# A convolution feeding a channel mix: the first x over two hardware queues, and the first two groups convolved together

## The chip, the cores and the metric

The kernel runs on one core of a Trainium2 chip. Each core has its own instruction streams: TensorE (PE, with its weight loads shown as PEld), VectorE (DVE), ScalarE (ACT), GpSimd (POOL) and SyncE (SP). SP, ACT and POOL can issue DMA transfers; those of SP and ACT are hardware queues, those of POOL a software queue, which can change the type of the data on the way. Matrix products go into PSUM, from where VectorE and ScalarE read them; the rest of the on-chip data lies in SBUF. The metric is the time of one execution on the device in microseconds (us), as a median over runs.

## The reference

`x` is 8 sequences of 4160 tokens with 192 channels, fp32. First a causal convolution over 7 tokens, whose weights are a softmax, one set for each of 8 heads of 24 channels; then a channel mix with a shift by one token.

```python
w = softmax(weight)                               # 8 heads x 7 taps
out = einsum('hk,bskhg->bshg', w, x_unfolded)     # causal, zeros ahead of token 0

x = out
x_prev = x shifted by one token, zeros first
xk = mu_k * x + (1.0 - mu_k) * x_prev
xr = mu_r * x + (1.0 - mu_r) * x_prev
k = np.maximum(xk @ w_k, 0.0)                     # 192 -> 1024
v = k * k @ w_v                                   # 1024 -> 192
r = 1.0 / (1.0 + np.exp(-(xr @ w_r)))
return r * v
```

## The kernel before

Sequences are worked on in four pairs. The tokens of a pair are cut into blocks of 120, and blocks into groups: in the first pair groups 0 to 5 have 3, 4, 4, 5, 10 and 9 blocks, and later pairs have larger ones. A group's life: `x_tile` takes a buffer `xb` out of three and clears what lies ahead of the first token; `load_x` loads it on POOL's queue and casts fp32 to bf16 on the way (lines 116 and 122); `conv` multiplies it with `toe`, a banded matrix for each head that holds the softmaxed weights (`conv_mm`, line 250), and copies the result out of PSUM to `y` (`conv_out`, lines 286 and 289). Then `y` must be turned so that channels lie on partitions: groups 0 to 3 by transposes on TensorE (`tr`, line 324) that VectorE copies to `yT` (line 334), the others by way of DRAM. Of `yT`'s three parts, two hold channels 0 to 127 of one sequence each, the third channels 128 to 191 of both.

The channel mix goes in steps of 512 tokens, the first one of 256. For a step, VectorE makes `diff` (line 355) and from it with `mix` the operand `xk` and later `xr` (lines 394 and 397: a product, then a sum). `k_mm` (line 416) multiplies `xk` with `wk` into PSUM tiles, one per slot: first the 128 high channels ("hi"), then the 64 low ones ("lo") of the two sequences. `k_relu` (line 457) on ScalarE reads a slot, `k_square` (line 476) on VectorE squares it, `v` (line 505) and `r` (lines 500, 501, 522) follow, and `v_out` multiplies and writes. The first step has four slots, the second eight; four slots are a bundle.

All PSUM tiles come from one `ring` of four, in the order in which they are asked for: a tile is used again only when its fourth predecessor has been read. Every engine works strictly in the order in which the program issues its instructions, and that order is written by hand: `prologue` (line 654) up to the first bundle, then the loop at line 710, which runs tables of functions (`early`, `first`, `xt`, `mixes`, `late` and others) entered by bundle number.

The prologue's order matters here. SP loads `w_raw`, the raw weights, then six small pieces of `mu`. POOL makes `ident`, issues the four transfers of group 0's x (lines 116 and 122), makes the mask `band`, and then issues group 1's x (two), `wk` (three, lines 158 to 160), group 2's x (two), `wr` (five), `wv` (line 170); two memsets follow (line 692), then x of groups 3 and 4. Each queue kind has eight semaphores for its transfers, so the ninth waits until the first has landed. VectorE and ScalarE turn `w_raw` into the softmax and `toe` (lines 173 to 224). ScalarE loads its table for Exp at the start (line 659) and the one for Sigmoid after it (line 179). TensorE runs `warm`, products of constants that nobody reads: 16 at first, then 4, 2 and 3 between the convolution of group 0 (8 products), its 9 transposes, and the convolution of group 1. Group 0's `y` is copied by `conv_out_first` in six pieces (lines 268 and 272).

In the first bundle the first two slots of K are computed (hi, then lo), then group 1 is transposed, then the other two slots follow; group 2 is convolved behind them, and K of the second step after that. In the second bundle come group 2's transposes and group 3's convolution.

Of the kernel before, what the change touches and what calls it, by code (L numbers as in the profile page):

```python
# [14 lines left out]
def kernel(  # L15
# [114 lines left out]


    w_raw = const.tile([P, H, K], FP32)
# [24 lines left out]
    def load_wk():  # L157
        nc.gpsimd.dma_start(out=wk[:, 0, :], in_=moe_w_k[0:P, :])
        nc.gpsimd.dma_start(out=wk[0:LO, 1, :], in_=moe_w_k[P:D, :])
        nc.gpsimd.dma_start(out=wk[LO:P, 1, :], in_=moe_w_k[P:D, :])  # L160
# [11 lines left out]
    def softmax():  # L172
        nc.vector.tensor_reduce(out=w_max, in_=w_raw, axis=mybir.AxisListType.X, op=ALU.max)
        nc.vector.tensor_tensor(
            out=w_exp, in0=w_raw, in1=w_max.unsqueeze(2).to_broadcast([P, H, K]), op=ALU.subtract
        )
        nc.scalar.activation(out=w_exp, in_=w_exp, func=AF.Exp)

        nc.scalar.activation(out=w_sig, in_=w_exp[:, 0, 0:1], func=AF.Sigmoid)
        nc.vector.tensor_reduce(out=w_sum, in_=w_exp, axis=mybir.AxisListType.X, op=ALU.add)  # L180
        nc.vector.reciprocal(out=w_sum, in_=w_sum)
        nc.vector.tensor_tensor(
            out=w_nrm,
            in0=w_exp,
            in1=w_sum.unsqueeze(2).to_broadcast([P, H, K]),
            op=ALU.mult,
        )
# [52 lines left out]
    def conv_mm(g, c):  # L240
        nb = groups[g][2]
        if c == 0 and g > 0:
            ys[g] = two.tile([P, GB, 2 * D], BF16, tag="y", name="y")
# [14 lines left out]
    def conv_out_first():  # L258

        nb = groups[0][2]  # L260
        ys[0] = [const.tile([P, nb, P], BF16, tag=f"y0{i}", name="y0") for i in range(3)]
        for c, hs in enumerate(chunks(0)):
            ps = conv_ps.pop((0, c))
            c0, c1 = hs[0] * G, hs[-1] * G + G
            n = min(c1, P) - c0
            if n > 0:
                for i, copy in enumerate((nc.scalar.copy, nc.vector.tensor_copy)):
                    copy(out=ys[0][i][:BLK, :, c0 : c0 + n], in_=ps[:BLK, :, i, 0:n])
            if c1 > P:
                n = c1 - max(c0, P)  # L270
                lo = ys[0][2][:BLK, :, :].rearrange("p n (s c) -> p n s c", s=2)
                nc.scalar.copy(out=lo[:, :, :, c1 - P - n : c1 - P], in_=ps[:BLK, :, :, c1 - c0 - n : c1 - c0])
# [41 lines left out]
    def tr(g, j):  # L314

        p, blk0, nb, _, _ = groups[g]
        if blk0 == 0 and j == 0:
            new_yT(p)
# [3 lines left out]
        for c in range(3):  # L322
            for i in todo:
                nc.tensor.transpose(
                    out=view[:, (i - 4 * j) // 2, c, i % 2, :],
                    in_=ys[g][c][:BLK, i, :] if g == 0 else ys[g][:BLK, i, c * P : (c + 1) * P],
                    identity=ident[:BLK, :BLK],
                )

        def evacuate(cs):  # L330
            for i in todo[::2]:
                n = min(2, nb - i)
                c0 = YC + (blk0 + i) * BLK
                nc.vector.tensor_copy(
                    out=yTs[p][:, cs, c0 : c0 + n * BLK].rearrange("p c (n t) -> p c n t", n=n),
                    in_=view[:, (i - 4 * j) // 2, cs, :n, :],
                )

        if g > 0:
            evacuate(slice(0, 3))  # L340
        else:
            for part, cs in enumerate((slice(0, 2), slice(2, 3))):
                evacuate(cs)
                diff(0, cs)
                mix(0, 0, part)
# [16 lines left out]
    def mix(s, i, part):  # L362
# [28 lines left out]
        else:  # L391
            sl = slice(0, 2) if part == 0 else slice(2, 3)
            o = t[:, sl, :L]
            nc.vector.tensor_scalar(  # L394
# [6 lines left out]
    def k_mm(n, hi, start):  # L401
# [5 lines left out]
        if start:  # L407
            k_ps[n] = ring.tile([P, 2, BANK], FP32, tag="k", name="ps_k")
# [15 lines left out]
    def k_section(ns):  # L424
# [4 lines left out]
        h = len(ns) // 2 if ns[0] > 0 else len(ns)  # L429
# [158 lines left out]
    def conv(g, c):  # L588
        conv_mm(g, c)
        for k in range(c, min(c + 2, len(chunks(g)))):  # L590
            conv_out(g, k, nc.scalar.copy)

    for g, (p, blk0, nb, fb, on_pe) in enumerate(groups):
        nx = -(-len(chunks(g)) // 2)
# [4 lines left out]
        elif p == 0:  # L599
            xs = {2: [0, 0], 3: [1, 1], 4: [2, 2, 3, 3], 5: [4, 4, 5, 5]}[g]  # L600
# [48 lines left out]
    def warm(n):  # L649
        ps = ring.tile([P, 2, BANK], FP32, tag="k", name="warm")  # L650
# [3 lines left out]
    def prologue():  # L654
# [3 lines left out]
        )  # L658
        nc.scalar.preload_act_table(AF.Exp)
        nc.vector.memset(ones_t, 1.0)  # L660
        x_tile(0, nc.vector)
        nc.vector.memset(zeros, 0.0)
        nc.gpsimd.affine_select(
# [8 lines left out]
        load_x(0)  # L672
        masks_band()

        warm(WARM)
        x_tile(1, nc.vector)
        x_tile(2, nc.vector)
        masks_mod8()
        nc.vector.memset(wr[:, 2:4, :], 0.0)
        softmax()  # L680
        make_toe()
        load_x(1)
        load_wk()
# [9 lines left out]
        for c in range(0, len(chunks(0)), 2):  # L693
            conv_mm(0, c)
        conv_out_first()
        warm(4)
        tr(0, 0)
        warm(2)
        for c in range(0, len(chunks(1)), 2):
            conv(1, c)  # L700
        warm(3)
# [3 lines left out]
    with tc.manual_schedule():  # L705
# [4 lines left out]
        for b in range(quads[-1][2] + 1):  # L710
            ns = bundles[b] if b < len(bundles) else ()
            run(early, b)
            for part in (ns[:2], ns[2:]) if b == 0 else (ns,):
# [4 lines left out]
                if part[:1] == ns[:1]:  # L718
# [40 lines left out]
```

## Time and profile before

| | |
|---|---|
| Time, median of 7 runs | 446.23 us (445.85 to 446.76) |
| The profiled execution | 446.53 us, of which 444.8 us are the span of the profile |
| Granted TensorE clock | 1.00 |
| ScalarE, relu of K (line 457) | 260 instructions, 245.9 us |
| TensorE, K (line 416) and V (line 505) | 191.6 and 179.4 us |
| Data moved | 63.64 MB, mean 143 GB/s |

The profile is one execution. Busy time counts what an engine works; the idle time in front of an instruction is put down to what released it. Matmuls are pipelined, so their times overlap. In a timeline, a line with "x4" is four instructions merged, with the start of the first. The trace also records when each transfer has landed. Those of the beginning, in us: group 0's x last at 7.07, group 1's x at 9.46 and 10.53, `wk` at 12.15, 12.95 and 13.70, group 2's x at 14.48 and 15.52, `wr` last at 16.45, `wv` at 19.38, group 3's x at 22.64 and 23.90. `w_raw` landed between 2.62 and 3.91 on the 16 DMA engines.

### The profile page before, as it was taken

The page shows a single profiled execution, that of the slowest core. Times are in us where ns is not written, and L with a number is a line of the kernel's source. Part 1 is how long each engine was busy: PE and PEld are TensorE (multiplying, and loading weights), DVE is VectorE, ACT ScalarE, POOL GpSimd, SP SyncE. Part 2 cuts the span into 40 slices and gives each one's busy share as a digit, 9 for nine tenths or more (in the row PEclk, how much of TensorE's full clock was granted, in tenths as well). Part 3 has the DMA queues.
Part 4 walks back from the last instruction along what each step waited for, and adds up shares of the span by engine and source line. Part 5 has one row for each costly group of instructions (what it writes and reads, how often), then busy time and mean ns, then how long its engine had stood idle before and what let it go on. Part 6 is the DMA issues. An engine that isn't in the chain of part 4 may idle for free.

```text
span 444.8 us, 9773 instructions
## 1 busy us (share of the span) xinstructions
PE 433.6 (97%) x3937; PEld 304.4 (68%) x3937; DVE 388.5 (87%) x705; ACT 353.7 (80%) x465; POOL 48.1 (11%) x70
## 2 busy tenths in 40 slices
PE   7879999999999999999999999999999999999996
PEld 3455766766867766676676776677676677666776
DVE  5889799889988999889979898889988898999973
ACT  3878888888897797889888788888889778777772
POOL 8650001102020100012020010010200000000000
PEclk9999999999999999999999999999999999999999
DMA  8998759989495693295899495466955553431123
GB/s 91 152 187 148 193 147 161 153 198 195 122 225 163 145 195 87 82 199 127 170 212 165 117 207 142 111 101 178 196 146 131 159 124 113 85 97 65 45 72 116
DMA packets 133231, 63.64 MB, mean 143 GB/s; under 512 B 84770, under 2 KB 132930, under 8 KB 133186
## 3 DMA queue, kind: packets, MB, share of 16 engines
q1 hardware_dynamic: 94594, 48.08, 41.0%
q0 software_dynamic: 38224, 14.68, 28.6%
q8 instruction: 31, 0.51, 0.5%
q10 hardware_dynamic: 368, 0.25, 0.2%
q14 instruction: 14, 0.11, 0.1%
HBM read 29.39 MB, written 36.99 MB: 149 GB/s over the span
## 4 chain that ended last, share of the span: by engine, by line
PE 88%; DVE 3%; DMA 3%; ACT 3%; POOL 2%; issue 1%
PE ps_k L416 37%; PE ps_v L505 37%; PE ps_r L501 4%; PE ps_r L500 4%; PE ps_c L250 4%; DMA xb<-in_x_dram 2%; DMA wk<-in_moe_w_k_dram 1%; ACT y L286 1%; POOL xb L122 1%; DVE k L476 1%; ACT r_sb L522 1%; PE ps_vt L505 1%; ACT k_sb L457 0%; DVE xk L397 0%; DVE o_sb L532 0%
## 5 line engine op out<-in xcount | busy, mean ns | idle before, releaser
L457 ACT ACTIVATE k_sb<-ps_k 128x1024 bf16<-128x1024 f32 x260 | 245.9, 1037 | 13.2 <-PE ps_k L416 10.0
L416 PE MATMUL ps_k<-xk,wk 64*128 64x512 bf16 (+3 forms) x1056 | 191.6, 373 | 2.7 <-DVE xk L397 1.8
L505 PEld LDWEIGHTS <-k 128*128 128x128 bf16 x2048 | 170.9, 98 | 14.9 <-issue 0.7
L505 PE MATMUL ps_v<-wv,k 128*128 128x192 bf16 x2048 | 179.4, 246 | 0.6 <-ACT k_sb L457 0.6
L476 DVE TENSOR_TENSOR k<-k_sb 128x1024 bf16<-128x1024 bf16 x256 | 168.2, 686 | 10.2 <-ACT k_sb L457 9.1
L416 PEld LDWEIGHTS <-wk 64*128 64x128 bf16 (+1 forms) x1056 | 66.5, 96 | 102.1 <-issue 55.8
L532 DVE TENSOR_TENSOR o_sb<-ps_v,r_sb 128x768 f32<-128x768 f32 x63 | 60.3, 957 | 24.0 <-PE ps_v L505 23.6
L522 ACT ACTIVATE r_sb<-ps_r 128x768 bf16<-128x768 f32 x64 | 53.1, 830 | 24.8 <-PE ps_r L501 24.8
L286 ACT CAST y<-ps_c 120x480 bf16<-120x480 f32 (+6 forms) x84 | 38.4, 515 | 33.4 <-PE ps_c L250 33.4
L122 POOL DMA_DIRECT2D xb<-in_x_dram x36 | 32.1, 897 | 169.7 <-PE ps_k L416 95.2
L500 PE MATMUL ps_r<-wr,xr 128*128 128x192 bf16 x256 | 47.4, 246 | 0.2 <-DVE o_sb L532 0.2
L501 PE MATMUL ps_r<-wr,xr 128*128 128x192 bf16 x256 | 47.4, 247 | 0.0
L397 DVE TENSOR_TENSOR xk<-xk,yT 128x1024 bf16<-128x1024 bf16 (+1 forms) x66 | 36.3, 549 | 2.3
L397 DVE TENSOR_TENSOR xr<-xr,yT 128x1024 bf16<-128x1024 bf16 (+1 forms) x66 | 36.2, 549 | 2.3
L250 PE MATMUL ps_c<-xb,toe 128*128 128x480 bf16 (+4 forms) x144 | 31.1, 322 | 2.1 <-DMA xb<-in_x_dram 1.8
L355 DVE TENSOR_TENSOR d<-yT 128x1536 bf16<-128x1536 bf16 (+4 forms) x38 | 31.8, 837 | 0.1
L394 DVE TENSOR_SCALAR xk<-d,mu 128x1024 bf16<-128x1024 bf16 (+1 forms) x66 | 27.6, 419 | 1.2
L501 PEld LDWEIGHTS <-xr 128*128 128x128 bf16 x256 | 25.1, 98 | 3.9 <-issue 0.5
L500 PEld LDWEIGHTS <-xr 128*128 128x128 bf16 x256 | 25.0, 98 | 3.6
L394 DVE TENSOR_SCALAR xr<-d,mu 128x1024 bf16<-128x1024 bf16 (+1 forms) x66 | 27.2, 412 | 0.0
L289 ACT CAST y<-ps_c 120x480 bf16<-120x480 f32 (+6 forms) x45 | 20.3, 502 | 8.0 <-PE ps_c L250 8.0
L250 PEld LDWEIGHTS <-toe 128*128 128x128 bf16 x144 | 12.7, 98 | 4.1 <-issue 2.2
(58 smaller groups left out, 80.3 us busy)
## 6 DMA issues: line engine op xcount, KB each, us to landing
out_dram<-o_sb SPq DMA_DIRECT2D x61, 384.0 KB, 3.2
y_dram<-y SPq DMA_DIRECT2D x10, 900.0 KB, 6.9
xb<-in_x_dram POOLq DMA_DIRECT2D x14, 480.0 KB, 8.8
xb<-in_x_dram POOLq DMA_DIRECT2D x6, 432.0 KB, 7.4
xb<-in_x_dram POOLq DMA_DIRECT2D x10, 192.0 KB, 6.4
y_dram<-y SPq DMA_DIRECT2D x3, 450.0 KB, 4.1
y_dram<-y SPq DMA_DIRECT2D x1, 810.0 KB, 5.7
xb<-in_x_dram POOLq DMA_DIRECT2D x2, 384.0 KB, 7.7
```

The costliest lines, as they stand in the source:

```text
L250: nc.tensor.matmul(out=ps[:, :, :, i * G : (i + 1) * G], lhsT=toe[:, h, :], rhs=xbs[g][:, :nb, :, h * G : (h + 1) * G], start=True, stop=True,
L286: copy(out=yh[:, :, :, c0 : c0 + n], in_=ps[:BLK, :, :, 0:n])
L394: nc.vector.tensor_scalar(out=o, in0=d[:, sl, :L], scalar1=mu[:, i, part : part + 1], scalar2=None, op0=ALU.mult)
L397: nc.vector.tensor_tensor(out=o, in0=o, in1=yT[:, sl, c0 : c0 + L], op=ALU.add)
L416: nc.tensor.matmul(out=ps[:, i, f * L : (f + 1) * L], lhsT=wk[r, 0 if hi else 1, fs], rhs=xk[r, i if hi else 2, :L], start=start and f == ...
L457: nc.scalar.activation(out=k_sb, in_=ps.rearrange("p a b -> p (a b)"), func=AF.Relu)
L476: nc.vector.tensor_tensor(out=o, in0=i, in1=i, op=ALU.mult)
L500: nc.tensor.matmul(out=o, lhsT=hi, rhs=wr[:, 0, :], start=True, stop=False)
L501: nc.tensor.matmul(out=o, lhsT=lo, rhs=wlo, start=False, stop=True)
L505: nc.tensor.matmul(out=o, lhsT=k2s[s][:, f, t * P : (t + 1) * P], rhs=wv[:, f, :], start=(f == 0), stop=(f == NF - 1),)
L522: nc.scalar.activation(out=r_sbs[s, j], in_=ps, func=AF.Sigmoid)
L532: nc.vector.tensor_tensor(out=o_sb.rearrange("p (b t) d -> p b (t d)", b=2), in0=v_ps.pop((s, j)), in1=r_sbs.pop((s, j)), op=ALU.mult,)
```

## The change

- Group 0's x is no longer loaded and cast by POOL. `load_x_first` loads it as fp32 into a tile `x_f32` (in a buffer of the tag that `k2` uses later), three transfers for one sequence on SP's queue behind `w_raw`, and three for the other on ScalarE's queue ahead of its first table load. VectorE clears the first 32 partitions of block 0 ahead of its other work. ScalarE casts both to bf16 with two copies, placed between Exp and Sigmoid.
- Groups 0, 1 and 2 are convolved by `conv_small`: 15 products in place of 8, one PSUM bank for each of the three parts of `yT`, and three copies in all (ScalarE, VectorE, ScalarE; for group 2 all by ScalarE).
- The order of TensorE becomes: 16 `warm`, convolution of groups 0 and 1, transposes of group 0 (`tr_first`, which evacuates with one copy of VectorE and one of ScalarE), transposes of group 1, 2 `warm`, then all of the first bundle's K. The fillers of 4, 2 and 3 are gone.
- The first `mix` of high and of low channels is one fused instruction each.
- POOL's order becomes: `ident`, `band`, x of group 1, `wk` in two halves of three transfers each, x of group 2, `wr`, `wv`, the memsets, x of group 3. Group 2 is convolved at one go behind the first bundle.

```diff
+    def load_x_first(s, eng):
+        nb = groups[0][2]
+        for q0, q1, n0, n1 in ((0, P, 1, nb), (16, P, 0, 1), (HALO, 16, 0, 1)):
+            eng.dma_start(
+                out=x_f32[q0:q1, n0:n1, s, :],
...
     def softmax():
...
         nc.scalar.activation(out=w_exp, in_=w_exp, func=AF.Exp)
+        xbs[0] = three.tile([P, GB, 2, D], BF16, tag="xb", name="xb")
+        for s in range(2):
+            nc.scalar.copy(out=xbs[0][:, : groups[0][2], s, :], in_=x_f32[:, :, s, :])
 
         nc.scalar.activation(out=w_sig, in_=w_exp[:, 0, 0:1], func=AF.Sigmoid)
...
+    def conv_small(g, copies):
+        nb = groups[g][2]
+        ys[g] = [two.tile([P, 4, P], BF16, tag=f"y_small{i}", name="y_small") for i in range(3)]
+        tiles = [ring.tile([P, 2, BANK], FP32, tag="k", name="ps_c") for _ in range(2)]
+        banks = [t[:, i, 0 : nb * P] for t, i in ((tiles[0], 0), (tiles[1], 0), (tiles[0], 1))]
+        for i, o in enumerate(banks):
+            o = o.rearrange("p (n s c) -> p n s c", n=nb, s=2 if i == 2 else 1)
+            c0, c1 = (P, D) if i == 2 else (0, P)
+            for h in range(c0 // G, -(-c1 // G)):
+                a, b = max(c0, h * G), min(c1, h * G + G)
+                nc.tensor.matmul(out=o[:, :, :, a - c0 : b - c0], lhsT=toe[:, h, :],
+                    rhs=xbs[g][:, :nb, slice(0, 2) if i == 2 else slice(i, i + 1), a:b],
...
+        for i, o in enumerate(banks):
+            copies[i](out=ys[g][i][:BLK, :nb, :].rearrange("p n c -> p (n c)"), in_=o[:BLK, :])
...
+    def tr_first():
...
+        nc.vector.tensor_copy(
+            out=yT[:, 0:2, YC : YC + n], in_=tiles[0][:, 0, 0 : 2 * n].rearrange("p (c t) -> p c t", c=2)
+        )
+        nc.scalar.copy(out=yT[:, 2, YC : YC + n], in_=tiles[1][:, 0, 0:n])
+        for part, cs in enumerate((slice(0, 2), slice(2, 3))):
+            diff(0, cs)
+            mix(0, 0, part)
...
             o = t[:, sl, :L]
+            if s == 0 and i == 0:
+                return go(o, sl, 0, P)
...
-        h = len(ns) // 2 if ns[0] > 0 else len(ns)
+        if ns[0] == 0:
+            k_ps[0] = ring.tile([P, 2, BANK], FP32, tag="k", name="ps_k")
+            run(first, 0)
+            warm(k_ps[0], 2)
+            for n in ns:
+                k_mm(n, True, True)
+            for n in ns:
+                k_mm(n, False, False)
+            return
+        h = len(ns) // 2 if ns[0] > 2 else len(ns)
...
+        nc.vector.memset(x_f32[0:32, 0, :, :], 0.0)
+        nc.vector.memset(ones_t, 1.0)
+        load_x_first(0, nc.sync)
+        load_x_first(1, nc.scalar)
         nc.scalar.preload_act_table(AF.Exp)
-        nc.vector.memset(ones_t, 1.0)
-        x_tile(0, nc.vector)
...
-        load_x(0)
         masks_band()
+        load_x(1)
+        load_wk(0, NF // 2)
...
-        load_x(1)
-        load_wk()
+        load_wk(NF // 2, NF)
         load_x(2)
...
-        for c in range(0, len(chunks(0)), 2):
-            conv_mm(0, c)
-        conv_out_first()
-        warm(4)
-        tr(0, 0)
-        warm(2)
-        for c in range(0, len(chunks(1)), 2):
-            conv(1, c)
-        warm(3)
+        conv(0, 0)
+        conv(1, 0)
+        tr_first()
         x_tile(3, nc.vector)
         load_x(3)
```

## The prediction

> **What bounds the kernel now.** I read the page first: span and engine table, then the row of TensorE in 40 slices.
>
> ```profile
> span 444.8 us, 9773 instructions
> PE 433.6 (97%) x3937; PEld 304.4 (68%) x3937; DVE 388.5 (87%) x705; ACT 353.7 (80%) x465; POOL 48.1 (11%) x70
> PE   7879999999999999999999999999999999999996
> ```
>
> TensorE is the bound, but not from the beginning: a slice is 11.1 us, and the first three are not full. So next the busy time by stretch (start:end, length, then busy us and instructions of PE, PEld, DVE, ACT, POOL; granted clock, DMA share, GB/s).
>
> ```profile
> 7.25:16.00 8.75, 7.72 (x74) 4.73 (x74) 4.94 (x16) 4.67 (x11) 6.97 (x13) 1.00 1.31 166
> 16.00:25.50 9.50, 6.37 (x58) 4.11 (x57) 9.22 (x21) 8.18 (x14) 5.55 (x8) 1.00 1.40 158
> 25.50:36.00 10.50, 9.40 (x84) 6.01 (x83) 9.36 (x18) 8.12 (x14) 3.95 (x5) 1.00 1.58 187
> 36.00:444.80 408.80, 404.75 (x3712) 287.57 (x3712) 360.85 (x639) 329.70 (x425) 25.54 (x32) 1.00 0.65 143
> ```
>
> From 36 us on PE is busy 404.75 of 408.80, and the idle rest is the tail, where the last slice's 6 stands. A change here can only shift the moment from which PE is full; whatever it shifts, the end gets. From 16 to 25.5 PE works 6.37 of 9.50 while VectorE (9.22) and ScalarE (8.18) are nearly full. What ends PE's and ScalarE's waits there is in the timeline (start, us, what, in brackets the idle time before and its releaser).
>
> ```profile
> 18.61 2.98 PE L416 MATMUL ps_k<-xk,wk 128*128 128x512 bf16 x16 [1.31 <-DVE xk L397]
> 24.03 0.98 PE L250 MATMUL ps_c<-xb,toe 128*128 128x240 bf16 x8 [1.82 <-DMA xb<-in_x_dram]
> 15.15 0.97 DVE L334 COPY yT<-ps_t 128x720 bf16<-128x720 bf16 x2 [1.44 <-PE ps_t L324]
> 14.20 3.77 ACT L457 ACTIVATE k_sb<-ps_k 128x1024 bf16<-128x1024 f32 x4 [1.24 <-PE ps_k L416]
> 20.01 3.77 ACT L457 ACTIVATE k_sb<-ps_k 128x1024 bf16<-128x1024 f32 x4 [0.46 <-PE ps_k L416]
> 24.64 1.35 ACT L286 CAST y<-ps_c 120x480 bf16<-120x480 f32 x3 [0.86 <-PE ps_c L250]
> 13.99 0.92 POOL L170 DMA_DIRECT2D wv<-in_moe_w_v_dram  x1 [0.24 <-DMA wk<-in_moe_w_k_dram]
> 15.83 3.66 POOL L122 DMA_DIRECT2D xb<-in_x_dram  x4
> ```
>
> Two chains meet at 24.64, where ScalarE begins to copy group 3's convolution. (a) POOL's queue: wv may be issued only when the last wk transfer is in (13.99), then two memsets, then group 3's x at 15.83; it lands at 23.90 and frees PE at 24.03. (b) ScalarE: first relu 14.20, four relus to 17.97, group 2's copies to 19.55, a wait of 0.46, four relus to 23.78. VectorE's block from 15.15 to 28.4 has no gap, so it only needs to begin earlier. From 24.64 the chain is ScalarE's copies, r_sb at 26.50, relus at 27.20. To move the end, both (a) and (b) must move.
>
> **The first x on hardware queues.** The first x landed at 7.07, and the first convolution at 7.25 waited for toe, not for x. So a faster x alone gives nothing; what counts is what leaves POOL's queue. Four issues go (0.72+0.75+0.57+0.72=2.76 us). Ahead of them the memset of x_f32 (384 elements; rows of 192 and 256 took 0.218 and 0.272, so about 0.38 against the 0.22 removed) moves to the front and delays ones_t, ident and zeros by 0.4 and 0.15, which the toe chain does not feel: VectorE idled 1.59 before w_max. ident then runs to 1.8, the band masks (4.31 to 4.98, 0.67) to 2.5, and group 1's x is issued at 2.55 instead of 4.92: 2.37 earlier. With the delays of before (4.5 and 4.9 from issue) it lands by 8.2, ahead of conv 1. wk now has six issues (6 x 0.56 = 3.3), to 7.35; group 2's x waits for group 1's first landing (7.1) and goes until 9.0; wr's five (0.53 to 0.61) until 11.9. The bytes ahead of wk's end are the same, so its last landing goes from 13.70 to 11.3. wv is issued at 11.9 to 12.9 (13.99 before), memsets to 13.9, and x of group 3 at 13.9 instead of 15.83: 1.9 to 2.0 earlier, landing at 21.9, conv 3 at 22.0.
>
> Bounds of this gain: 2.9 (POOL never waits for a landing), and nothing, if the transfers ahead are held by the DMA engines alone. I take 2.0, since the releaser before wv is wk's landing, which moves.
>
> Hardware x: 756 packets, fp32, 566 KB, three issues on SP behind w_raw (0.39 to 0.6 each, 1.2 to 2.9) and three on ScalarE (0.8 to about 2.4; the table load follows to 3.7, and Exp is due only at 4.43). Landing, from below: SP's smallest pieces took 2.9 from issue, so 5.2; from above: the pace of the software queue (283 KB from 3.7 to 7.07) for twice the bytes gives 8.8. The nearest row is SP's 384 KB store of 512 such rows, 3.2 us; I take 5.6. mu's last five issues wait on SP for hardware landings (a semaphore is used again), but the two that the low mix needs at 12.3 are out by 6.8 and land by 10 (2.9 to 3.2 from issue), the rest serves xr, after 21 us. What is at stake beside it is w_raw: it shares the engines with x and may land later by 0 to 0.7 (its own 3.1 us, of which 1.3 is spread over landings); I take 0.3, which goes straight into toe and K.
>
> **The casts.** Two copies of 576 elements; no such row, nearest 480 (0.565) and 1024 (1.04), so 0.65 each. ScalarE: x 5.6, casts to 6.9, then the Sigmoid table load, which before sat in the shadow at 4.69 (1.28), to 8.2, w_sig (0.20) to 8.4. Queued behind them are group 0's copies, due at 8.05: 0.4 late, but conv 1 fills PE until 9.3 anyway. A landing later than 5.6 is paid only in part.
>
> [...]
>
> **Convolution back to back.** Each of groups 0 and 1 has 15 matmuls instead of 8; at 0.055 (transposes of 120 columns stand that far apart: 12 in 0.80 with 0.23 of pipeline) they end at 8.5 and 9.3, starting at 7.25 and held by toe's second half until 7.65. Copies: ScalarE 8.45 to 9.3 (two of 384, 0.42 each back to back as three took 1.14), then 9.3 to 10.4 (two of 512); VectorE 8.35 to 8.9 and 9.4 to 10.1 (216 and 168 elements took 0.383 and 0.332, so 1.06 ns an element). Transposes of group 0 from 9.3 to 10.0, of group 1, which before stood between K's halves at 14.31, to 11.1. yT: one copy of 720 (0.5) from 10.2 to 10.7; the rest by ScalarE to 10.8. diff 0.43 to 11.15; mix is now one fused instruction instead of 0.35+0.43. Its rows are 64 elements 0.278 and 128 0.350, so 0.78 for 512 and 0.49 for 256: no gain on the first, 0.1 on the second (bounds: 0.43, the two-operand row, and 0.8). xk at 11.9 (12.41 before); diff and mix of the low part to 12.75 (13.71).
>
> Now group 1's transposes are there already: VectorE goes on at 12.75 instead of 15.15, which is 2.4 earlier, as 1.44 of waiting and 1.0 of lateness vanish; K of step 1 moves from 18.61 to 16.2. ScalarE's first relu follows the low xk by 0.49 (13.71 to 14.20), so 13.25 instead of 14.20. Its chain is then full: relus to 17.0, group 2's three copies (3 x 0.55) to 18.65, relus to 22.4 (23.78), with the 0.46 of waiting gone. With 0.3 for w_raw: 22.7. The warm-up matmuls removed (9, some 0.21 each) and the extra 7 in group 2's convolution lie where PE idles.
>
> **The sum.** Copies of group 3 start at the later of ScalarE 22.7 and conv 3's 22.0 plus 0.6: 22.7 instead of 24.64, 1.9 less. Behind it r_sb, K, transposes and PE's full stretch follow in the old order. The profiled execution took 446.53 (span 444.8 and 1.73 around it), which makes 444.6; it stands 0.3 above the median of 446.23, which I shift alike: 444.3.
>
> **Rivals.**
> 1. ScalarE late: x or the table switch holds its copies. If x lands at 8.8, casts, load and w_sig end at 11.6, yT at 12.7, K's low part at 14.7 (1.0 later than before), while VectorE still goes on 0.4 earlier; some 0.3 is left: 445.9. For: the Sigmoid load moves behind the casts. Against: no hardware transfer here took over 3.2 + 1.
> 2. Group 3's x lands at 23.9 as before. Then conv 3 stays and all else is hidden: 446.2. For: DMA share is above 1 from 7 to 30 us. Against: until 4 us nearly no engine moves data, and that is when x goes now.
> 3. Slower: PE's clock falls. The first warm-up matmuls stand 0.43 apart, the last ones 0.21, so the clock opens only with work, and the fillers between 8 and 12 us go. Place: 9.3 to 12, where only transposes and two fillers run. Price: at half rate four slots of K at step 0 take 5.1 instead of 2.56 and pass ScalarE's 3.8 by 1.3; at step 1 6.0 by 2.2: 3.5, less 1.9, 447.8. It decides once half rate costs more than 1.9. Against: PE idled 1.31 and 1.82 at a stretch, and its 16 matmuls at 18.61 still took 2.98; the longest idle I expect now is 1.4.
>
> **How the numbers follow.** Forecast 0.80, from 443.1 to 445.3: a gain of 2.8 if w_raw is not delayed, the fused mix costs 0.43 and POOL never waits, with 0.3 for the measurement, down to 1.0. Rival 1 0.06, rival 2 0.06, rival 3 0.08. The range goes to 446.0: left out are rival 3, half of rival 2 and 0.05 below. What this measurement can tell from no change is about 0.2%, 0.9 us, so faster means below 445.3: the forecast, 0.80. Within it are rivals 1 and 2 but for 0.01: 0.11. Slower: rival 3 and that 0.01, 0.09.
>
> **What would show it.** Right: group 3's x issued near 13.9 and conv 3 near 22; first relu near 13.5; VectorE without a gap from about 13; copies of group 3 near 22.7; PE full from some 34. Wrong: w_max later than 4.3; ScalarE's first y copy past 9; matmuls of K at step 0 twice as far apart; conv 3 still waiting at 24 for x.

## The result, and the profile after

| | before | changed |
|---|---|---|
| median | 446.5 us (445.39 to 447.64, 40 runs) | 445.2 us (444.59 to 445.91, 17 runs) |
| ratio to the kernel before | | 0.9973, 95% interval 0.9966 to 0.998 |
| profiled execution | 446.53 us, span 444.8 | 445.25 us, span 443.5 |

The medians are 1.3 us apart; by the ratio the change gains 1.2 us (0.27% of 446.5). Two later series of the same program, one a copy and one with an edit that did nothing, gave 0.9982 and 0.9991, a gain of 0.8 and 0.4 us, while the median of the kernel before moved between 445.85 and 446.5 from series to series. So where a difference is below half a microsecond, I read it from the profiles and put the ratio beside it. The profiles have a spread too: in the three of this one program the first relu comes at 14.08, 14.31 and 14.32, and the copies of group 3 at 23.16, 23.14 and 23.31. Differences of 0.2 between profiles are not read as effects.

First the page of the changed kernel: span, engine table and TensorE's 40 slices.

```profile
span 443.5 us, 9796 instructions
PE 432.9 (98%) x3951; PEld 304.3 (69%) x3951; DVE 388.7 (88%) x700; ACT 354.0 (80%) x461; POOL 47.1 (11%) x69
PE   7889999999999999999999999999999999999996
```

PE's third slice rose from 7 to 8, and nothing else moved: as expected, only the front of the span is at stake. The table by stretch (busy us and instructions of PE, PEld, DVE, ACT, POOL, then granted clock, DMA share, GB/s) says what happened in it.

```profile
7.25:16.00 8.75, 7.08 (x92) 4.99 (x92) 6.94 (x16) 5.93 (x11) 6.78 (x12) 1.00 1.27 158
16.00:25.50 9.50, 7.58 (x67) 4.27 (x64) 9.33 (x21) 9.33 (x16) 5.90 (x8) 1.00 1.47 170
25.50:36.00 10.50, 9.40 (x84) 5.97 (x81) 9.21 (x18) 7.83 (x12) 3.09 (x4) 1.00 1.59 191
```

Between 7.25 and 16 us VectorE works 6.94 instead of 4.94: its block now begins earlier. From 16 to 25.5 PE is busy for 7.58 instead of 6.37, and ScalarE for 9.33 of 9.50 instead of 8.18. ScalarE has no room left there. The granted clock stays at 1.00 throughout. The timeline has the rows that answer to those shown of before (start, us, what, in brackets the idle time before and its releaser), and then those of the first microseconds.

```profile
17.90 2.82 PE L455 MATMUL ps_k<-xk,wk 128*128 128x512 bf16 x14 [0.33 <-ACT k_sb L506]
22.55 0.98 PE L271 MATMUL ps_c<-xb,toe 128*128 128x240 bf16 x8 [1.20 <-DMA xb<-in_x_dram]
13.27 0.96 DVE L358 COPY yT<-ps_t 128x720 bf16<-128x720 bf16 x2
14.08 3.77 ACT L506 ACTIVATE k_sb<-ps_k 128x1024 bf16<-128x1024 f32 x4 [2.18 <-PE ps_k L455]
19.13 3.86 ACT L506 ACTIVATE k_sb<-ps_k 128x1024 bf16<-128x1024 f32 x4
23.16 1.35 ACT L313 CAST y<-ps_c 120x480 bf16<-120x480 f32 x3 [0.17 <-PE ps_c L271]
13.36 0.99 POOL L188 DMA_DIRECT2D wv<-in_moe_w_v_dram  x1
15.22 3.71 POOL L122 DMA_DIRECT2D xb<-in_x_dram  x4
...
4.52 0.21 DVE L191 TENSOR_REDUCE w_max<-w_raw 128x8 f32<-128x56 f32 x1 [2.00 <-DMA w_raw<-in_weight_dram]
6.34 1.25 ACT L198 CAST xb<-x_f 128x576 bf16<-128x576 f32 x2 [1.07 <-DMA x_f<-in_x_dram]
7.61 1.28 ACT L200 ACT_TABLE_LOAD   x1
8.90 0.20 ACT L200 ACTIVATE w_sig<-w_exp 128x1 f32<-128x1 f32 x1
9.79 0.63 PE L291 MATMUL ps_c<-xb,toe 128*128 128x96 bf16 x9 [0.66 <-DMA xb<-in_x_dram]
8.98 0.79 POOL L122 DMA_DIRECT2D xb<-in_x_dram  x1 [1.71 <-DMA xb<-in_x_dram]
```

Both chains moved, and chain (a) sets the size. ScalarE copies group 3's convolution from 23.16 instead of 24.64: 1.48 earlier. In (a), PE begins conv 3 at 22.55 instead of 24.03, the moment that x lands: the same 1.48. Group 3's x was issued 0.61 earlier, and it landed 7.2 us behind that issue (22.42) where it had taken 8.1 (23.90); why it then landed faster is not shown. In (b), ScalarE's second relus end at 22.99 (19.13 + 3.86) instead of 23.78, 0.79 earlier, which is enough to be out of the way: ScalarE still waits for PE, by the row for 0.17. (ScalarE's copies can start before the relus ahead of them have ended: in `e7_x3_ahead_wr` below, where they wait for nothing, they start 3.62 behind the start of those relus, which take 3.86. So here ScalarE could have begun at 22.75, and group 3's x costs 0.41.) VectorE's block starts at 13.27 instead of 15.15 and shows no wait. Those 1.48 are carried unchanged past 36 us (K's matmuls of 35.41 stand at 33.93), shrink to 1.3 at the end of the span, and to 1.2 in the ratio.

The last six rows show what came later than reckoned: `w_max` at 4.52 (3.93 before), the casts at 6.34, and above all group 1's x, whose second half lets PE go on at 9.79 only. POOL feels the same landing: the issue of group 2's x waits for it until 8.98, and everything behind it in POOL's queue with it.

### The profile page after: what moved, and what is told of

It reads as the page before. It is cut to its first block, busy times and chain, and to the rows that moved or that the text cites. A ratio compares the mean times of both kernels' runs of the same rounds, so it can differ in the third digit from the quotient of the medians.

```text
span 443.5 us, 9796 instructions
## 1 busy us (share of the span) xinstructions
PE 432.9 (98%) x3951; PEld 304.3 (69%) x3951; DVE 388.7 (88%) x700; ACT 354.0 (80%) x461; POOL 47.1 (11%) x69
## 4 chain that ended last, share of the span: by engine, by line
PE 88%; DVE 4%; DMA 3%; ACT 3%; issue 1%; POOL 1%
PE ps_k L455 38%; PE ps_v L554 37%; PE ps_r L549 4%; PE ps_r L550 4%; PE ps_c L271 4%; DMA xb<-in_x_dram 3%; ACT y L313 1%; DVE k L525 1%; ACT r_sb L571 1%; PE ps_vt L554 1%; DVE d L392 0%; DVE xk L436 0%; ACT k_sb L506 0%; DVE o_sb L581 0%; DVE xk L433 0%
## 5 line engine op out<-in xcount | busy, mean ns | idle before, releaser
L525 DVE TENSOR_TENSOR k<-k_sb 128x1024 bf16<-128x1024 bf16 x256 | 168.2, 686 | 10.2 <-ACT k_sb L506 9.1
L313 ACT CAST y<-ps_c 120x480 bf16<-120x480 f32 (+4 forms) x78 | 36.1, 518 | 31.5 <-PE ps_c L271 31.5
L122 POOL DMA_DIRECT2D xb<-in_x_dram x34 | 30.7, 908 | 171.8 <-PE ps_k L455 95.2
L271 PE MATMUL ps_c<-xb,toe 128*128 128x480 bf16 (+2 forms) x120 | 28.6, 338 | 1.2 <-DMA xb<-in_x_dram 1.2
L316 ACT CAST y<-ps_c 120x480 bf16<-120x480 f32 (+4 forms) x41 | 18.9, 509 | 8.0 <-PE ps_c L271 8.0
L271 PEld LDWEIGHTS <-toe 128*128 128x128 bf16 x120 | 10.9, 98 | 2.2 <-issue 1.3
```

The lines of the kernel that those rows point to most:

```text
L271: nc.tensor.matmul(out=ps[:, :, :, i * G : (i + 1) * G], lhsT=toe[:, h, :], rhs=xbs[g][:, :nb, :, h * G : (h + 1) * G], start=True, stop=True,
L313: copy(out=yh[:, :, :, c0 : c0 + n], in_=ps[:BLK, :, :, 0:n])
L525: nc.vector.tensor_tensor(out=o, in0=i, in1=i, op=ALU.mult)
```

## The experiments

### One part of the change alone

**The new order, with x on POOL as before.** `e1_x_on_pool` is the changed kernel without the hardware transfers.

```diff
-        nc.vector.memset(x_f32[0:32, 0, :, :], 0.0)
-        load_x_first(0, nc.sync)
-        load_x_first(1, nc.scalar)
+        x_tile(0, nc.vector)
...
+        load_x(0)
         masks_band()
...
-        for s in range(2):
-            nc.scalar.copy(out=xbs[0][:, : groups[0][2], s, :], in_=x_f32[:, :, s, :])
```

> The changed kernel with the first x back on POOL's queue (four issues ahead of the masks, cast on the way) and no casts on ScalarE; the new order of TensorE stays. My theory: the hardware queues matter because they free POOL. Here group 1's x is issued at 5.2 instead of 2.38 and lands near 10.8 instead of 9.74; convolution of group 1, which now stands ahead of the first transposes, waits for it, K of step 0 begins near 13.8 instead of 12.68, and group 3's copies on ScalarE near 24.4 (23.16 in the changed kernel, 24.64 before): ratio to before 0.9995 (0.998 to 1.001). Rival, the new order alone is the gain: ratio 0.997 as in the changed kernel, copies of group 3 near 23.2.

Measured: 446.02 us, ratio 1.0003 (0.9986 to 1.002), with single runs from 444.87 to 447.82. Three rows of its timeline, PE's, ScalarE's and POOL's, and then its table by stretch:

```profile
24.74 1.76 PE L268 MATMUL ps_c<-xb,toe 128*128 128x240 bf16 x8 [2.68 <-DMA xb<-in_x_dram]
25.73 1.35 ACT L310 CAST y<-ps_c 120x480 bf16<-120x480 f32 x3 [2.04 <-PE ps_c L268]
16.55 3.72 POOL L122 DMA_DIRECT2D xb<-in_x_dram  x4
```

```profile
22.00:24.70 2.70, 0.06 (x2) 0.00 (x0) 2.63 (x8) 1.69 (x2) 2.12 (x4) 0.93 1.57 186
24.70:27.70 3.00, 2.96 (x17) 2.47 (x18) 2.85 (x6) 1.97 (x5) 0.78 (x1) 0.50 1.60 192
27.70:30.00 2.30, 2.14 (x14) 0.74 (x14) 0.00 (x0) 1.81 (x4) 2.11 (x3) 0.99 1.60 191
```

POOL issues group 3's x at 16.55, later than the kernel before (15.83), because the four issues of group 0's x and six of wk are now ahead of it. PE waits 2.68 for it, and the granted clock (the column behind POOL's) halves: 0.50 from 24.70 to 27.70. The eight matmuls of conv 3 take 1.76 where they took 0.98, and three microseconds at half rate lose 1.5. That is the mechanism of my third rival, at a place where I had not looked for it. In this execution, then, what POOL's shorter queue gives to the change is an x of group 3 that comes early enough, for ScalarE and for the clock.

But this execution is the slowest of the ten runs. The three whose mean granted clock was 1.0 took 444.87, 445.04 and 445.67, as long as the changed kernel; the seven at 0.996 took 445.69 to 447.82. With x landing as late as in the profile, even at full clock the copies would come behind conv 3's 24.74 and so behind the 24.64 of the kernel before; those three runs must have had it earlier, and no trace shows them. So x on POOL loses the gain in most runs, but that it loses anything where the clock holds is not shown.

**The hardware x, in the old order.** `e2_hw_x_only` is the kernel before with only this:

```diff
+        nc.vector.memset(x_f32[0:32, 0, :, :], 0.0)
+        load_x_first(0, nc.sync)
+        load_x_first(1, nc.scalar)
         nc.scalar.preload_act_table(AF.Exp)
...
-        x_tile(0, nc.vector)
-        load_x(0)
...
+        for s in range(2):
+            nc.scalar.copy(out=xbs[0][:, : groups[0][2], s, :], in_=x_f32[:, :, s, :])
```

> The kernel before with only the first x moved to the two hardware queues and cast by ScalarE; wk whole, order of TensorE as before. My theory: ScalarE's chain binds, so that a free POOL queue gives little: w_raw lands 0.6 later, the first relu comes at 14.6 to 15 instead of 14.20, group 3's x lands near 21.5 but its copies on ScalarE begin only near 24.3: ratio 0.9995 (0.998 to 1.001). Rival, POOL's queue alone decides: copies of group 3 near 22.3, ratio 0.995.

Measured: 447.83 us, ratio 1.0044 (1.0028 to 1.0059): clearly slower, and by far more than expected. Its timeline, ScalarE, then VectorE and POOL, and PE's first convolution:

```profile
8.93 0.32 ACT L288 CAST y<-ps_c 120x216 bf16<-120x216 f32 x1
15.93 3.77 ACT L477 ACTIVATE k_sb<-ps_k 128x1024 bf16<-128x1024 f32 x4 [2.12 <-PE ps_k L436]
25.20 1.39 ACT L306 CAST y<-ps_c 120x480 bf16<-120x480 f32 x3
13.97 1.15 DVE L414 TENSOR_SCALAR xk<-d,mu 128x256 bf16<-128x256 bf16 x1
14.03 1.01 POOL L713 MEMSET tail<- 128x512 bf16 x2
7.79 0.89 PE L270 MATMUL ps_c<-xb,toe 128*128 128x144 bf16 x8 [0.71 <-DVE toe L244]
```

Group 3's x landed at 22.16, 1.7 earlier than before, and it is of no use: ScalarE's copies are at 25.20 behind its own relus. The first relu is 1.73 late (15.93 against 14.20), and two rows account for it. The first copy out of PSUM stands behind the casts and the Sigmoid load, 8.93 instead of 8.05, which is 0.88; of these, 0.54 would be there without them, since the late `w_raw` lets the first convolution begin at 7.79 instead of 7.25, and 0.34 is theirs. The product for the low part of xk takes 1.15 instead of the 0.29 that the same instruction took before, which is 0.86: it runs beside POOL's memset of `tail` and ends as that ends. So about half of the lateness is a meeting with a memset, and not the price of the casts; this order with the memsets elsewhere was not tried. The copies are 0.56 late, PE's full stretch 0.81 (V of the first step at 30.98 instead of 30.17), and the span 1.2; what adds the rest is not shown. In this order nothing covers ScalarE's new work. By the medians, neither half of the change gains anything by itself; the new order covers the casts, and the hardware x keeps group 3 in time for the new order. The other parts (`conv_small`, the fused mix, the fillers) were not taken out one by one.

**The transposes of group 1 put back between K's halves.** `e12_tr1_behind` moves one line of the changed kernel.

```diff
             k_ps[0] = ring.tile([P, 2, BANK], FP32, tag="k", name="ps_k")
-            run(first, 0)
             warm(k_ps[0], 2)
...
                 k_mm(n, False, False)
+            run(first, 0)
```

> The changed kernel with one line moved: the transposes of group 1 stand behind the first half of K, as in the kernel before, and no longer ahead of K. Theory (the gain is the earlier start of VectorE's unbroken block, which needs group 1's transposes ahead of K): the transposes run at about 14.2 us, VectorE waits some 1.3 for them and goes on at 14.7 in place of 13.27, K of step 1 starts at 18.8 in place of 17.90, the second four relus at 20.2 in place of 19.13, group 3's copies at 23.8 in place of 23.16, the ratio to the kernel before 0.9995 (0.9985 to 1.0005). Rival (the order of conv 1 and group 3's loads made the loss of the kernel with group 0 transposed first, not this line): ScalarE's chain is unchanged from the second relus on, group 3's copies at 23.2 to 23.4, ratio 0.998.

Measured: 445.67 us, ratio 0.9995 (0.9986 to 1.0004).

```profile
15.01 0.97 DVE L358 COPY yT<-ps_t 128x720 bf16<-128x720 bf16 x2 [1.68 <-PE ps_t L349]
18.29 2.98 PE L455 MATMUL ps_k<-xk,wk 128*128 128x512 bf16 x16 [1.09 <-DVE xk L436]
19.69 3.77 ACT L506 ACTIVATE k_sb<-ps_k 128x1024 bf16<-128x1024 f32 x4
23.59 1.35 ACT L313 CAST y<-ps_c 120x480 bf16<-120x480 f32 x3
22.98 0.98 PE L271 MATMUL ps_c<-xb,toe 128*128 128x240 bf16 x8 [1.09 <-DMA xb<-in_x_dram]
```

VectorE waits 1.68 again and goes on at 15.01 (15.15 before the change), K of step 1 is set by VectorE at 18.29, and the copies follow at 23.59, 0.43 later than in the changed kernel. Up to the second relus (19.69 instead of 19.13) the theory holds, at about half the size expected. The 0.43 at the copies is not proof of it: they start 0.61 behind conv 3, as in the changed kernel, and conv 3 is 0.43 late because group 3's x landed at 22.85 instead of 22.42, though POOL issued it at the same time (15.21, 15.22). By its relus alone ScalarE could have begun near 23.3, which is 0.56 later than in the changed kernel but only some 0.2 later than its copies. So the early transposes of group 1 are worth about 0.2 at the copies, as an estimate from these rows; the ratio fell by more, 0.0013 to 0.0022, and what else takes part in that is open.

### What the hardware transfers cost the others

`e3_no_first_x` leaves group 0's x unloaded.

```diff
-        load_x_first(0, nc.sync)
-        load_x_first(1, nc.scalar)
...
+        nc.vector.memset(x_f32[:, :, 0, :], 0.0)
+        nc.vector.memset(x_f32[:, :, 1, :], 0.0)
```

> The changed kernel without the six hardware transfers of the first x: x_f32 is cleared by VectorE instead, so group 0 is computed from zeros. It shows what these transfers cost the others. My theory, they hold up w_raw and group 1's x: w_raw in by 3.95 (w_max at 4.52 in the changed kernel), group 1's x by 7.5 and 8.6 (8.70 and 9.74), group 2's x issued at 7.5 instead of 8.98, copies of group 3 near 22.1: ratio to before 0.9945 (0.9935 to 0.996). Rival, the software queue sets its own pace: w_raw earlier alike, but group 1's x at 8.5 and 9.5 again, conv 1 at 9.6, copies of group 3 near 23, ratio 0.997.

Measured: 442.81 us, ratio 0.993 (0.9913 to 0.9947).

```profile
3.92 0.21 DVE L191 TENSOR_REDUCE w_max<-w_raw 128x8 f32<-128x56 f32 x1 [0.71 <-DMA w_raw<-in_weight_dram]
7.24 1.72 PE L291 MATMUL ps_c<-xb,toe 128*128 128x72 bf16 x30 [0.91 <-DVE toe L245]
6.79 0.87 POOL L122 DMA_DIRECT2D xb<-in_x_dram  x1
21.29 1.48 ACT L313 CAST y<-ps_c 120x480 bf16<-120x480 f32 x3
```

Without those transfers `w_max` is back at 3.92, both convolutions run in one go from 7.24, POOL issues group 2's x at 6.79 with no wait, and the copies stand at 21.29. Group 1's x landed at 6.37 and 7.59, which is 4.4 and 4.7 us from its issues and so the delay that I had forecast for the change; in the changed kernel it took 6.3 and 6.5. The front of the changed kernel could be 1.87 earlier still. The hardware transfers therefore held up `w_raw` by 0.6 and group 1's x by 1.9 and 1.8. (Two other things moved with them: ScalarE's wait for x is gone, and without the clearing of `x_f32` ahead of `ident` POOL's queue starts 0.4 earlier, with group 1's x at 1.98 instead of 2.38. So the 1.87 is the price of the whole load, not of the sharing alone.)

`e5_w_raw_first` and `e6_x1_ahead_masks` tried to win some of it back by order of issue.

```diff
-        load_x_first(1, nc.scalar)
         nc.scalar.preload_act_table(AF.Exp)
+        load_x_first(1, nc.scalar)
```

> The changed kernel with ScalarE's three x transfers issued behind its table load (near 2.1 instead of 0.80), so that w_raw has the queues to itself. My theory now: convolution of group 1 waits for group 1's x, which binds the first half of the chain, so an earlier toe is not paid. w_max near 4.0 instead of 4.52, first convolution at 7.3 instead of 7.84, but group 1's convolution again at 9.8 and the first relu near 14.1: ratio 0.997. Rival, the toe chain binds: everything behind it 0.5 earlier, first relu near 13.6, ratio 0.996.

Measured: 445.38 us, ratio 0.9991 (0.998 to 1.0001). This tells nothing about its question: the transfers were still issued at 0.84, because the queue did not wait for the table load (0.81 to 2.09), and `w_raw` landed at 4.49 as in the changed kernel. It stands as a repeat: copies at 23.31.

```diff
-        masks_band()
         load_x(1)
+        masks_band()
```

> The changed kernel with group 1's x issued ahead of the two band masks on POOL, at 1.8 instead of 2.38. My theory, its landing follows its issue: 8.1 and 9.1 instead of 8.70 and 9.74, convolution of group 1 at 9.2, first relu near 13.5, group 2's x issued at 8.4, group 3's copies near 22.6: ratio 0.996. Rival, the 16 DMA engines are held by the hardware x until 6.2, whatever the issue: landing within 0.2 of 9.74, ratio 0.9973.

Measured: 445.06 us, ratio 0.9978 (0.9968 to 0.9987), no gain over the changed kernel beyond the spread of its own series (0.9973 to 0.9991).

```profile
5.78 0.21 DVE L191 TENSOR_REDUCE w_max<-w_raw 128x8 f32<-128x56 f32 x1 [3.25 <-DMA w_raw<-in_weight_dram]
1.77 1.66 POOL L122 DMA_DIRECT2D xb<-in_x_dram  x2
9.09 1.72 PE L291 MATMUL ps_c<-xb,toe 128*128 128x72 bf16 x30 [2.34 <-DVE toe L245]
```

Issued 0.61 earlier, group 1's x landed 0.38 earlier (8.32 and 9.36), but `w_raw` 1.25 later, at 5.75. The convolutions then ran in one go, from 9.09, and the first relu came at 14.46 instead of 14.08. One lateness replaced the other.

### POOL's queue, and which chain binds

`e4_wk_whole` loads wk in three transfers again, ahead of group 2's x.

```diff
-        load_wk(0, NF // 2)
+        load_wk(0, NF)
...
-        load_wk(NF // 2, NF)
```

> The changed kernel with wk loaded in three transfers again, all ahead of group 2's x. Group 2's x then needs no semaphore used before, so POOL's stall of 1.71 at 8.98 goes. My theory, two chains tie at 23: group 3's x is issued near 14.2 instead of 15.22 and lands near 21.5, its convolution no longer waits for it, but ScalarE is in its relus until 22.99, so only 0.17 is won: ratio 0.9969. Rival, POOL's queue is the only bound: 1.0 is won, ratio 0.995.

Measured: 445.31 us, ratio 0.9984 (0.9974 to 0.9993). The 1.71 of waiting ahead of group 2's x is gone, but wr now waits 1.98, 0.71 and 0.55 in its place, and group 3's x is issued at 15.30. The copies are at 23.46, behind ScalarE's relus: group 1's x landed at 9.45 and 10.45, 0.7 later than in the changed kernel, and with it the first relu, at 14.79. Here POOL's wait for a landing moved along its queue; this order of issues did not take it away.

`e7_x3_ahead_wr` issues group 3's x ahead of wr and wv, so that chain (a) can't bind.

```diff
         load_x(2)
+        conv(0, 0)
+        conv(1, 0)
+        x_tile(3, nc.vector)
+        load_x(3)
         load_wr()
...
-        conv(0, 0)
-        conv(1, 0)
         tr_first()
-        x_tile(3, nc.vector)
-        load_x(3)
```

> The changed kernel with group 3's x issued directly behind group 2's, ahead of wr and wv. It takes the wait for group 3's x away. My theory, two chains tie near 23: x of group 3 lands near 17.5 instead of 22.42, its convolution waits for nothing, but ScalarE's relus end at 22.99 again and the copies of group 3 begin there instead of at 23.16: ratio 0.997. Rival, the landing of group 3's x alone sets the end: 1 us or more earlier, ratio below 0.9955.

Measured: 445.13 us, ratio 0.9983 (0.9973 to 0.9992).

```profile
21.37 0.57 PE L271 MATMUL ps_c<-xb,toe 128*128 128x240 bf16 x4
19.30 3.86 ACT L506 ACTIVATE k_sb<-ps_k 128x1024 bf16<-128x1024 f32 x4
22.92 1.48 ACT L313 CAST y<-ps_c 120x480 bf16<-120x480 f32 x3
```

Group 3's x landed at 17.57 and 18.83 instead of 22.42, PE no longer waits for it, and the copies come at 22.92, right behind the relus of 19.30. 3.6 us less on one chain are worth 0.24 (0.41, had the relus come at 19.13 as in the changed kernel): the two chains were tied within half a microsecond. Further on even that is gone: V of the second step stands at 36.31, against 36.29 in the changed kernel.

`e8_both` has the edits of both `e6_x1_ahead_masks` and `e7_x3_ahead_wr`.

> Group 1's x ahead of the masks and group 3's x ahead of wr and wv, together. My theory: with the wait for group 3's x gone, whatever group 1's x gains on ScalarE's chain is paid in full, up to 0.6: group 3's copies near 22.4, ratio 0.9957. Rival, group 1's landing does not follow its issue: as the run with group 3's x moved alone, 0.997.

Measured: 445.35 us, ratio 0.9982 (0.9973 to 0.9992); `w_raw` 5.48, first relu 14.19, copies 23.10. No gain: the rival's outcome, but not for its reason. Group 1's x did follow its issue (8.07 and 9.09 instead of 8.70 and 9.74); `w_raw` came 1.0 later in exchange, and VectorE's product for step 1 took 1.71 instead of 0.49 beside POOL's last issue and memset.

### Group 0's transposes ahead of conv 1

If group 1's late x is what holds the first relu, the work that doesn't need it can go first. Three kernels in one series: the changed kernel as it is, the new order, and that order with the Sigmoid ahead of the casts. In the new order ScalarE also makes all three copies of group 1's convolution.

> The changed kernel once more, as the baseline for the two kernels beside it. From its first profile: conv 1 at 9.79 us, K at 12.68, first relu at 14.08, group 3's copies at 23.16, the ratio to the kernel before 0.9973 (0.996 to 0.999).

```diff
-            run(first, 0)
             warm(k_ps[0], 2)
...
+            run(first, 0)
...
-            return conv_small(g, (act_, dve_ if g < 2 else act_, act_))
+            return conv_small(g, (act_, dve_ if g < 1 else act_, act_))
...
+        conv(0, 0)
+        x_tile(3, nc.vector)
+        load_x(3)
         load_wr()
         load_wv()
...
-        conv(0, 0)
+        tr_first()
         conv(1, 0)
-        tr_first()
-        x_tile(3, nc.vector)
-        load_x(3)
```

> The changed kernel with group 3's x issued ahead of wr and wv, and with group 0 transposed ahead of conv 1, so that the wait for group 1's x (9.74 us) stands behind those transposes and not ahead of them. Group 1's transposes come behind the first half of K. Theory (the late landing of group 1's x sets the first relu, and the relus set group 3's copies): yT of group 0 starts at about 9.9 in place of 10.87, K at 11.8 in place of 12.68, the first relu at 13.2 in place of 14.08, group 3's copies at about 22.3, the ratio 0.9955. Rival (mu's low pieces, landed at 12.25, or VectorE's copies for group 1, now behind the first xk, take it back): K or the relus stand as in the changed kernel, copies at 22.9 or later, ratio 0.9975.

```diff
+        nc.scalar.activation(out=w_sig, in_=w_exp[:, 0, 0:1], func=AF.Sigmoid)
         xbs[0] = three.tile([P, GB, 2, D], BF16, tag="xb", name="xb")
...
-        nc.scalar.activation(out=w_sig, in_=w_exp[:, 0, 0:1], func=AF.Sigmoid)
```

> The same as the kernel beside it, with the Sigmoid of w_exp ahead of the two casts, so that its table load (1.28 us) lies in ScalarE's wait for x. Theory: if the first copy out of PSUM (9.01 us, right behind the load and the Sigmoid) still holds up the front once conv 1 is out of the way, it starts some 0.3 us earlier and so does the first relu: 12.9, ratio 0.995. Rival: the casts, which end at 7.6 in the changed kernel, move behind the load to 8.5 or later, because w_max is there only at 4.7, and the conv of group 0 with them: no gain or a loss against the kernel beside it, ratio 0.9955 to 0.997.

Measured: 444.98 us, ratio 0.9982 (0.9969 to 0.9994) for the changed kernel; 445.81, 1.0001 (0.9991 to 1.0012) for the new order; 445.96, 1.0006 (0.9996 to 1.0016) with the Sigmoid first. Of the new order the timeline shows PE, ScalarE twice, VectorE and POOL:

```profile
12.05 1.65 PE L455 MATMUL ps_k<-xk,wk 128*128 128x256 bf16 x16 [0.52 <-DVE xk L412]
13.53 1.94 ACT L506 ACTIVATE k_sb<-ps_k 128x1024 bf16<-128x1024 f32 x2 [0.82 <-PE ps_k L455]
23.62 1.39 ACT L313 CAST y<-ps_c 120x480 bf16<-120x480 f32 x3
14.48 0.97 DVE L358 COPY yT<-ps_t 128x720 bf16<-128x720 bf16 x2 [1.44 <-PE ps_t L349]
16.48 1.32 DVE L433 TENSOR_SCALAR xk<-d,mu 128x1024 bf16<-128x1024 bf16 x1
16.45 1.08 POOL L748 MEMSET tail<- 128x512 bf16 x2
18.59 2.98 PE L455 MATMUL ps_k<-xk,wk 128*128 128x512 bf16 x16 [1.93 <-ACT y_small L299]
```

The theory was right on the first relu: 13.53 instead of 14.08, or of 14.31 in the profile taken beside it (13.2 was expected). The rival was right on the outcome. VectorE now waits 1.44 for group 1's transposes, as before the change, and then its product for step 1 takes 1.32 instead of 0.49, beside POOL's memset again. What is won at the first relu is lost again and more by the copies (23.62, against 23.14 beside it). PE idles 1.93 ahead of K, and 3 of 12 runs were granted 0.996 (4 of 12 with the Sigmoid first, 1 of 12 of the changed kernel, none of 29 of the kernel before in this series); that this idle time cost them their clock is likely, not shown. It is not the whole loss: the nine other runs have a median of 445.76. With the Sigmoid first, the first copies come 0.28 earlier (8.90 instead of 9.18), but the first relu only 0.02: the low xk product waits for `mu` until 12.53, which was 12.56. Of the loss, the memset's 0.83 and the wait for the transposes can't be separated here; the same order with the memsets elsewhere was not tried. An estimate from the rows: with the product at 0.49, K would start near 17.8, the second relus 1.41 behind it as here, and the copies near 22.8, some 0.3 ahead of the changed kernel. So the order itself may be a gain. Among the runs that load all of x, none beats the changed kernel by more than the series differ.

## Why the prediction was right, and where it was off

- **What bounds.** Right. Only the front moved; two chains met at group 3's copies, and both had to move. `e2_hw_x_only` shows it from one side (x in time, ScalarE late: a loss) and `e1_x_on_pool` from the other (ScalarE early, x late in its profile: nothing).
- **The size.** 444.3 was forecast, 445.2 measured, 0.1 inside the 445.3 that ended the forecast; the two later series of the same program show gains of 0.8 and 0.4 where I had 1.9. The copies start at 23.16 instead of my 22.7: 0.46 of the miss. Another 0.2 of the 1.48 is lost between 36 us and the end of the run, where I let the shift pass whole. The rest, 0.27, is the kernel before: its median was 446.5 in the series of the comparison, not 446.23.
- **The step that was off: group 1's landing.** I gave its transfers the delay of before, 4.5 and 4.9 us from issue. They took 6.3 from POOL's first issue to the first landing (2.38 to 8.70). I had asked what hardware x does to `w_raw`, not what it does to the software queue beside it. `e3_no_first_x` gives the delays that I used, 4.4 and 4.7, without those transfers. The late landing acts on both chains. In (b) follow conv 1 at 9.79, yT at 10.87 (10.2 forecast) and the first relu at 14.08 (13.55 with the 0.3 for `w_raw`).
- **POOL's queue.** I had it reach group 3's x at 13.9; it was 15.22. The 1.71 ahead of group 2's x, a wait for that same landing, is larger than that difference of 1.32. The transfer made up 0.8 of it (7.2 us from issue to landing, for the 8.0 I had taken from before), so conv 3 was at 22.55, not 22.0. This chain, which I had put 0.1 ahead of the other, is the one that set the copies: 22.55 and 0.61 make 23.16.
- **ScalarE's chain, right by luck.** I had it ready at 22.7, and it was ready at 22.75 (19.13 + 3.62), but two errors cancel: the first relu was 0.53 late, and relus, copies and relus took 3.63 + 1.42 + 3.62 = 8.67 where I had added up 9.2, because I had priced ScalarE's instructions to their end, and here the next one started before that (3.62 behind the start of relus that take 3.86, in `e7_x3_ahead_wr`).
- **w_raw.** 0.3 was taken, out of 0 to 0.7; it was 0.6 (4.52 against 3.93).
- **Casts and table.** Two casts 1.25 (1.3 forecast), the load 1.28, `w_sig` 0.01 behind its end (8.90). ScalarE was 0.6 late at its first copy (9.01 against 8.45), of which x's landing (6.27 instead of 5.6) is the cause, and it was covered, as I had said: conv 1 ran longer. That x took 4.4 to 4.7 us from issue also breaks what I held against rival 1, that no hardware transfer took over 4.2; the kernel before has some that do (the 900 KB stores of `y` take 6.9).
- **The fused mix.** 0.75 and 0.48, for 0.78 and 0.49 forecast from smaller rows.
- **K of step 1.** Forecast 16.2; VectorE had xk ready at 16.48, but the first two matmuls ran at 16.98 and the others from 17.90: PE waits for ScalarE to empty PSUM, not for VectorE. It cost nothing, since ScalarE's relus follow each other without a wait, but the forecast overlooked the ring of four.
- **Rivals.** ScalarE did not bind by the casts in the changed kernel, though in the old order it does. Group 3's x came 1.48 earlier, not as before. While PE had work to do, the clock did not fall in the profiled run, whose longest PE idle was 1.20; it did fall in `e1_x_on_pool`, where PE was left waiting 2.68, so the rival priced something that happens, at another place. Two of 22 later runs of the changed program had a mean clock of 0.995 (447.30 and 447.43 us); no trace shows where.

## What to carry to other kernels

Moving the first x from the software queue to the hardware queues shortened POOL's queue here (group 3's x was issued 0.61 earlier), but beside that load `w_raw` landed 0.6 later and group 1's x 1.9 and 1.8 later than without it (`e3_no_first_x`): price the landings of every neighbour, not only of the small one on the critical path. Where two chains end at the same instruction, test each half of a change alone before believing in either; here, by the medians, neither gains, one loses 0.44%, and together they gain 0.27%. Before calling a chain the one that sets the end, compare its shift with the shift of what follows: here 1.48 and 1.48 for the landing of group 3's x, 0.79 for ScalarE's relus. And an order that lets the first result come earlier need not gain: in `e10_tr0_ahead` the first relu came 0.78 earlier than in the profile beside it, but VectorE got through its long block later, and the copies came 0.48 later (23.62 against 23.14).

## What the hardware showed that I had not expected

- **Half clock after less than three microseconds of idling.** In `e1_x_on_pool` PE was idle for 2.68 us up to 24.74, and the granted clock was 0.50 from 24.70 to 27.70. It fell while PE was still idle: a mean of 0.93 over 22.00 to 24.70 puts the fall about 0.4 before 24.70 (0.07 of 2.70, over 0.5), some 2.3 us after PE's last matmul, an estimate from these rows. The same time does not bring it down everywhere: in `e6_x1_ahead_masks` PE was idle for 2.34 up to 9.09, and the granted clock was 1.00 from 9.00 to 10.00. At the end of the changed kernel's span it fell some 3.0 us after the last matmul (439.86; a mean of 0.83 over 442.50 to 443.00 and 0.50 behind it), and in the kernel before it was still 1.00 at 444.80, 3.5 us after the last one (441.26). In the kernels with a longest idle of 1.93 and 1.78 in their profiles 3 and 4 of 12 runs had a lower mean clock; how long PE idled in those runs themselves is not recorded.
- **A product on VectorE that took longer beside POOL's work.** TENSOR_SCALAR took 1.15 instead of 0.29 (256 elements, `e2_hw_x_only`) and 1.71, 1.32, 1.18 and 0.99 instead of 0.49 (1024 elements, `e8_both`, `e10_tr0_ahead`, `e11_tr0_sig` and `e1_x_on_pool`) where POOL's memset of `tail` ran at the same time. It is not the memset alone: in the changed kernel 0.75 instead of 0.35 (512 elements, at 16.40) and in the kernel before 0.67 instead of 0.49 (at 17.16) ran while POOL issued transfers. But a TENSOR_TENSOR of 1536 elements beside that memset kept its 0.96 in the changed kernel (14.27, the memset at 14.28). Beside the issues of transfers (3.71 us for four in the changed kernel) VectorE lost 0.40 and 0.18 in these two rows, 0.59 in `e6_x1_ahead_masks` (0.94 for 512 elements, at 16.78), and nothing in `e12_tr1_behind` (0.49 for 1024 elements, at 17.02). What decides between them is not shown.
- **A small hardware transfer that landed later beside both kinds of load.** `w_raw` (issued at 0.8 in every kernel) landed at 3.90 with only group 1's x on POOL beside it (issued at 1.98), at 4.50 with hardware x too (POOL's at 2.38), and at 5.75 and 5.48 when POOL's was issued 0.6 earlier beside hardware x. The software queue alone, even as early as 1.58 in the kernel before, left it at 3.91. Why 0.6 earlier costs 1.0 to 1.25 beside the hardware x stays open.
- **A DMA issue behind a table load on ScalarE that did not wait for it.** In `e5_w_raw_first` the load ran from 0.81 to 2.09, and the first issue behind it went out at 0.84 all the same.
